# Decay attention into a gated convolution: 64-token state updates on 64x64 tiles, three whole chunks first, weights widened 128 columns at a time, and one written-out order

## The chip, the cores and the metric

The kernel runs on one core of a Trainium2 chip. The metric is device time in microseconds (us) of one execution; lower is better. The engines are named as in the profile: PE (TensorE matmul) with PEld (its weight loads), DVE (VectorE), ACT (ScalarE), POOL (GpSimd) and SP (SyncE, whose queue issues all the DMAs here).

## The reference, cut to what matters

Input: q, k, v of 4 batches x 8 heads x 768 tokens x 64 (float32), one decay `lam` per head, and a gated layer with two 512x512 float64 weights and a 5-tap float64 convolution. Tokens go in blocks of 64:

```
for b in range(nb):                                   # 12 blocks of 64
    intra = einsum('bhic,bhjc->bhij', qb, kb) * Dmask # lam**(i-j) where i >= j, else 0
    intra = einsum('bhij,bhjd->bhid', intra, vb)
    inter = einsum('bhid,bhde->bhie', qb * lam_pow, kv_state)
    out[:, :, sl] = intra + inter
    kv_state = lam_block * kv_state + einsum('bhsd,bhse->bhde', kb * rev_pow, vb)
x = out, heads side by side                           # 4 x 768 x 512
gate = sigmoid(5-tap causal convolution of x along the tokens)
result = (gate * (x @ w_val)) @ w_out
```

## The kernel before, in words

A chunk `i` is 128 tokens of two batches (`NB2`), all 8 heads. There are 12 chunks, 6 for each pair of batches; a pair's first chunk starts from an empty state and its last need not update it. For each chunk:

- **Loads** (L348): four parts of 512 KB (q and k transposed to head rows, heads 0 to 3 and 4 to 7; then v and k by token), two parts to a DMA, or one for chunk 0.
- **Scaling**: `scale_k` multiplies k by its decay (on ACT, L411, for the chunks in `K_ACT`, else on POOL, L414); `scale_q` multiplies q by the powers in `qdec` (POOL, L422).
- **scores** (L453): for each half `u` of the heads, k by q. The 128x128 triangle is cut: a 64x128 strip and a 64x64 block per head and batch, so 16 matmuls per half, on the four 64x64 tiles of the array. `mask` (DVE, L467 or L465) multiplies the scores by `dmask`.
- **intra** (L509): masked scores by v into `xp` (PSUM), in two turns; between the turns ACT reads eight columns of `xp` (`peek`, L526) and the second turn waits for that. **inter** (L489): state by scaled q into the same `xp`, 16 matmuls of 128 columns, ahead of intra.
- **outer** (L538): k by v over the 128 tokens, 16 matmuls on 128x64 tiles, into `st`; `update` (DVE, L545/L547) adds `st` and the faded state `sdec`; `fade` (POOL, L550) makes `sdec` with the power of 128.
- `keep` (ACT, L569) copies `xp` to `x` in SBUF. `x` is split into two float32r terms: `x_hi` (ACT) and `x_lo` (DVE L597 for chunks 0 and 1, else POOL L602).
- **Gate**, for two chunks together: 4 groups of 128 columns, each one tap on ACT (L629) and four on DVE (L631) in a PSUM bank, then the sigmoid (ACT, L636).
- **value** (L667): per half 24 float32r matmuls of 256 columns (w_hi by x_hi, w_hi by x_lo, w_lo by x_hi). Up to chunk 5 ACT copies the result to SBUF (L676) and DVE multiplies by the gate there (L680); from chunk 6 (`DIRECT`) DVE reads PSUM. The product `h` is split by ACT (L702) and POOL (L705).
- **project** (L728): per batch 12 matmuls of 512 columns; ACT evicts (L736), SP stores (L739).

The float64 weights are taken apart and put together as float32 by `widen`, four times on [128, 1024]: DVE cuts out exponent (L270) and mantissa (L276), ACT scales three pieces (L281, L286, L290), DVE sets the sign (L293), POOL adds (L300), DVE multiplies (L303), ACT rounds the high term (L308), POOL subtracts for the low one (L311).

Every step is given to a `Plan` with an engine, an assumed duration, a rank and its buffers. `Plan.order` plays the steps against these durations and so fixes the order in which each engine's instructions are issued; each engine's queue and SP's keep that order on the chip. PSUM has eight banks: two for the scores, two for `xp`, four (`u`) shared by everything else.

## Time and profile before

| | |
|---|---|
| runs | 231.48, 228.76, 230.7 us; median 230.7 us |
| span of the profiled execution | 228.2 us |
| PE busy | 208.8 us (91%), 3070 matmul instructions |
| DVE / ACT / POOL busy | 149.8 / 118.6 / 126.5 us |
| read from HBM, written | 29.39 MB, 6.29 MB |

The span runs from the first to the last instruction; the time of the profiled execution itself is not listed apart from the runs, which lie 0.6 to 3.3 us over its span (the median 2.5). Busy time of PE is modelled: its matmuls overlap, so start-to-start times say more than mean durations.

### The profile page before, as it was taken

To read this page: it belongs to the slowest core of one execution; us is meant where nothing else is said; L and a number is where in the kernel's file an instruction comes from. 1 tells how busy PE (TensorE), PEld (TensorE's weight loads), DVE (VectorE), ACT (ScalarE), POOL (GpSimd) and SP (SyncE) were. 2 spreads that over 40 slices of the span, in tenths; PEclk is the share of its full clock that TensorE was granted. 3 is DMA by queue.
4 is the path that set the end of the run, shared out by engine and by line. 5 is a ranking of instruction groups with operands and counts; after the bars stand their busy time and mean duration, and the time that the engine had idled before them with its cause. 6 is when DMAs were issued, how large, how long until landed. Compare 5 with 4: busy or idle time off the path is not lost.

```text
span 228.2 us, 6926 instructions
## 1 busy us (share of the span) xinstructions
PE 208.8 (91%) x3070; PEld 187.0 (82%) x3070; DVE 149.8 (66%) x201; ACT 118.6 (52%) x214; POOL 126.5 (55%) x93
## 2 busy tenths in 40 slices
PE   6786969999899999988999997989998999999994
PEld 6676868989799989987877876969897899999884
DVE  5546787999999579995389899999117931111100
ACT  2239896767945915448275356757253634121222
POOL 2045985795266599799999493343180616222210
PEclk9657879999999999999999999999999999999999
DMA  5999999928298064927121121002111111111122
GB/s 148 407 422 422 426 378 388 339 73 336 45 360 322 19 214 178 350 57 316 47 95 46 49 92 50 3 13 84 46 46 49 47 46 46 49 46 46 49 92 92
DMA packets 8238, 36.13 MB, mean 158 GB/s; under 512 B 1168, under 2 KB 1424, under 8 KB 4880
## 3 DMA queue, kind: packets, MB, share of 16 engines
q1 hardware_dynamic: 8208, 35.68, 41.1%
q8 instruction: 24, 0.39, 0.7%
q14 instruction: 6, 0.05, 0.1%
HBM read 29.39 MB, written 6.29 MB: 156 GB/s over the span
## 4 chain that ended last, share of the span: by engine, by line
PE 49%; DVE 29%; DMA 9%; POOL 6%; issue 4%; ACT 2%; SPq 0%; ACTq 0%; DVEq 0%; POOLq 0%
PE op L728 22%; PE vp L667 20%; DVE acc L631 15%; DMA ld<-in_qkv 9%; DVE g L680 6%; DVE A L467 4%; POOL qd L422 3%; POOL w_m L300 2%; PE xp L509 2%; PE xp L489 2%; PE s L453 1%; DVE state L547 1%; DVE w_m L303 1%; DVE w_m L276 1%; PE st L538 1%
## 5 line engine op out<-in xcount | busy, mean ns | idle before, releaser
L631 DVE SCALAR_TENSOR_TENSOR acc<-x,conv_sb,acc 128x512 f32<-128x512 f32 x96 | 66.4, 748 | 8.4 <-ACT acc L629 8.2
L728 PE MATMUL op<-wo_hi,hs 128*128 128x512 f32 (+1 forms) x200 | 61.5, 390 | 2.3 <-ACT seen L526 1.0
L667 PE MATMUL vp<-x_hi,wv_hi 128*128 128x256 f32 x192 | 54.7, 285 | 0.5 <-ACT g L636 0.5
L667 PE MATMUL vp<-x_lo,wv_hi 128*128 128x256 f32 x192 | 53.7, 280 | 0.3 <-POOL x_lo L602 0.2
L667 PE MATMUL vp<-x_hi,wv_lo 128*128 128x256 f32 x192 | 53.6, 279 | 0.0
L705 POOL TENSOR_TENSOR hs<-g,hs 128x512 fp32r<-128x512 f32 x24 | 32.4, 1359 | 33.7 <-ACT hs L702 30.2
L728 PEld LDWEIGHTS op<-wo_hi,hs 128*128 128x128 f32 x200 | 35.8, 188 | 10.2 <-ACT seen L526 1.1
L602 POOL TENSOR_TENSOR x_lo<-x,x_hi 128x1024 fp32r<-128x1024 f32 x10 | 24.4, 2444 | 27.9 <-ACT x_hi L593 27.9
L728 PE MATMUL op<-wo_lo,hs 128*128 128x512 f32 (+1 forms) x100 | 38.6, 386 | 0.0
L667 PEld LDWEIGHTS vp<-x_hi,wv_hi 128*128 128x128 f32 x192 | 36.0, 187 | 2.2 <-ACT g L636 1.0
L422 POOL TENSOR_TENSOR qd<-ld,qdec 128x512 f32<-128x512 f32 x20 | 30.2, 1526 | 12.7 <-DMA ld<-in_qkv 12.7
L667 PEld LDWEIGHTS vp<-x_lo,wv_hi 128*128 128x128 f32 x192 | 36.1, 188 | 1.2 <-POOL x_lo L602 0.7
L736 ACT COPY o<-op 128x512 f32<-128x512 f32 (+1 forms) x25 | 14.2, 569 | 43.8 <-PE op L728 34.5
L667 PEld LDWEIGHTS vp<-x_hi,wv_lo 128*128 128x128 f32 x192 | 36.0, 188 | 0.0
L680 DVE TENSOR_TENSOR g<-vp,g 128x512 f32<-128x512 f32 x12 | 8.3, 688 | 35.4 <-PE vp L667 30.4
L509 PE MATMUL xp<-A,ld 64*64 64x128 f32 (+1 forms) x768 | 25.2, 262 | 2.4 <-ACT seen L526 1.8
L509 PEld LDWEIGHTS xp<-A,ld 64*64 64x64 f32 x768 | 21.4, 144 | 5.4 <-ACT seen L526 2.3
L467 DVE TENSOR_TENSOR A<-s,dmask 128x768 f32<-128x768 f32 x21 | 20.0, 951 | 9.0 <-PE s L453 7.6
L636 ACT ACTIVATE g<-acc 128x512 f32<-128x512 f32 x24 | 14.4, 600 | 16.8 <-DVE acc L631 16.8
L453 PE MATMUL s<-ld 64*64 64x128 f32 (+1 forms) x672 | 19.0, 252 | 4.0 <-DMA ld<-in_qkv 2.5
L728 PEld LDWEIGHTS op<-wo_lo,hs 128*128 128x128 f32 x100 | 18.8, 188 | 4.2
L453 PEld LDWEIGHTS s<-ld 64*64 64x64 f32 x672 | 17.0, 138 | 4.9 <-DVE A L467 1.7
(59 smaller groups left out, 264.1 us busy)
## 6 DMA issues: line engine op xcount, KB each, us to landing
ld<-in_qkv SPq DMA_DIRECT2D x22, 1024.0 KB, 7.9
out<-o SPq DMA_DIRECT2D x23, 256.0 KB, 2.0
ld<-in_qkv SPq DMA_DIRECT2D x4, 512.0 KB, 6.3
w_raw<-in_w_val SPq DMA_DIRECT2D x2, 1024.0 KB, 12.4
w_raw<-in_w_out SPq DMA_DIRECT2D x2, 1024.0 KB, 12.3
...
lam_bc<-in_lam SPq DMA_DIRECT2D x1, 8.0 KB, 1.7
```

The lines of the kernel that those rows point to most:

```text
L422: nc.gpsimd.tensor_tensor(out=s["qd"][:, hs], in0=lds[i]["qT"][:, u], in1=qdec[:, hs], op=ALU.mult)
L453: nc.tensor.matmul(s["s"][b][rows(r if lo == 0 else 1 - r), at(n)], t["kT"][rows(b), u, 2 * r + n, lo:hi], t["qT"][rows(b), u, 2 * r + n, ...
L467: nc.vector.tensor_tensor(out=s["A", u], in0=s["s", u], in1=m[:, None, :].to_broadcast([P, NB2, SW]), op=ALU.mult)
L509: nc.tensor.matmul(s["xp"][rows(n), b, h // 2, lo:], lds[i]["v"][rows(r), b, h * D : (h + 1) * D], s["A", u][rows(r), b, at(n)], start=fir ...
L602: nc.gpsimd.tensor_tensor(out=s["x_lo"], in0=s["x"], in1=s["x_hi"].bitcast(F32), op=ALU.subtract)
L631: nc.vector.scalar_tensor_tensor(out=to, in0=src, scalar=w, in1=to, op0=ALU.mult, op1=ALU.add)
L636: nc.scalar.activation(xu[un]["g"][:, ct].rearrange("p u (b i) -> p b u i", b=NB2), xu[un]["acc", ct].rearrange("p b (u i) -> p b u i", u= ...
L667: nc.tensor.matmul(vp[:, f, :], w[:, ct, fs], xx[:, ct, :], start=n_mm == 0, stop=n_mm == 3 * NT - 1,)
L680: nc.vector.tensor_tensor(out=gs(u), in0=val, in1=gs(u), op=ALU.mult)
L705: nc.gpsimd.tensor_tensor(out=s["h_lo"][:, us], in0=gs(u), in1=s["h_hi"][:, us].bitcast(F32), op=ALU.subtract,)
L728: nc.tensor.matmul(op[:, cols], hh[:, ft, ts], w[:, ft, cols], start=n_mm == 0, stop=n_mm == 3 * NT - 1,)
L736: nc.scalar.copy(s["o", b, j][:, cols], s["op", b, j][:, cols])
```

## The change

The `Plan` with durations and ranks gives way to one list, `ORDER`, of 697 step names that all engines follow. In it the first half of w_val is loaded ahead of chunk 0. Five matmuls of 512 columns on a tile of zeros are added (`f.0` to `f.4`: two at the start, two ahead of chunk 0's scores, one at the very end).

Chunks 0 to 2 (`BIG`) are computed whole: 128x128 scores, the half above the diagonal multiplied by zeros of the mask, 128 tokens in one state update. The other nine work by 64 tokens: 32 score matmuls of 64x64x64, 32 of intra, two halves of inter with 16 each, 32 of outer, all on 64x64 tiles, and two state updates and two fades. The scan for `qdec` on DVE becomes seven doublings on POOL; `kdec` is dropped; `dmask` is copied out of the 128-wide mask by ACT. `peek` stays in chunk 6 alone. Chunk 0's `scale_k` moves from ACT to POOL, and the pairs' last chunks (5 and 11), which had none, get `scale_k` (POOL), half an outer, one update.

`widen` runs on [128, 512], eight times; its sum moves from POOL to DVE and into a PSUM bank, and ACT's scaling of the low word is dropped. value is issued in four steps for each chunk and project in two for each batch. From chunk 6 the gated product stays in PSUM (`H_DVE`) and its low term moves from POOL to DVE. `keep` and the early `x_hi`, `x_lo` become two instructions each.

```diff
-SLOTS = {..., "A": 3, ...}
-K_ACT = (0, 1, 2, 3, 4, 6)
-S_OWN = (0, 1, 2)
+FILL = 5
+SLOTS = {..., "A": 2, ...}
+K_ACT = (1, 2, 3, 4, 6)
+BIG = (0, 1, 2)
+H_DVE = (6, 7, 8, 9, 10, 11)
+ORDER = """
+f.0 f.1 wv.0 dm.0 qe dm.1 ld.0.0 wv.0.1.e wv.0.0.e ld.0.2 wv.1 wv.0.0.m wv.0.1.m wv.0.0.w wv.0.1.w wv.0.0.r kd.0
+wv.0.0.s f.2 f.3 s.0.0 wv.0.1.r m.0.0.0 m.0.1.0 wv.0.0.v s.0.1 m.0.1.1 m.0.0.1 wv.0.1.s wv.0.1.v wv.1.0.e ia.0.0
+ia.0.1 wv.1.1.e st.0 up.0.0 ld.1.0 s.1.1 qd.1.0 wv.0.0.h wv.0.0.l dc wv.0.1.h ld.2.0 xh.0 xl.0 x.0 wv.0.1.l fd.0.0
+m.1.1.1 qd.1.1 qd.2.1 wv.1.0.r s.1.0 m.1.0.1 m.1.1.0 m.1.0.0 wv.1.0.m wv.1.0.w wv.1.0.s s.2.1 s.2.0 wv.1.0.v wv.1.1.m
+ld.1.2 ia.1.0 ia.1.1 kd.1 wv.1.1.w in.1.0 xh.1 m.2.1.1 wv.1.0.h wo.0 m.2.0.1 wo.0.1.e wo.0.0.e wo.0.1.r cv wv.1.0.l
+m.2.0.0 cv.e cv.m wv.1.1.r cv.r st.1 hi.0 xl.1 x.1 v.0.0 up.1.0 v.0.1 wv.1.1.s wv.1.1.v v.1.0 pb.0.0 v.1.1 m.2.1.0
...
+"""
     def run(self):
-        for k in self.order():
+        for name in ORDER.split():
...
+    def make_qdec():
+        nc.gpsimd.tensor_copy(qdec_c[:, :, 0:1], lam_bc[:, :, None])
+        n = 1
+        while n < C:
+            nc.gpsimd.tensor_tensor(
+                out=qdec_c[:, :, n : 2 * n], in0=qdec_c[:, :, 0:n],
+                in1=qdec_c[:, :, n - 1 : n].to_broadcast([P, H, n]), op=ALU.mult,
+            )
+            n *= 2
...
         def float_m():
+            s["v"] = bank("w_v", [P, n]) if big else const.tile([P, n], F32, name="w_v")
+            nc.scalar.activation(s["v"], s["m"], AF.Copy, bias=1.0, scale=2.0**-20)
...
         def whole():
-            nc.gpsimd.tensor_tensor(out=s["mf"], in0=s["mf"], in1=s["r"], op=ALU.add)
+            nc.vector.scalar_tensor_tensor(
+                out=s["v"], in0=s["low"].bitcast(U32), scalar=2.0**-52, in1=s["v"], op0=ALU.mult, op1=ALU.add
+            )
         def scale():
+            s["w"] = hi if not big else s["v"] if lo_dve else s["m"].bitcast(F32)
+            nc.vector.tensor_tensor(out=s["w"], in0=s["v"], in1=s["e"].bitcast(F32), op=ALU.mult)
...
+                for k in range(W_S):                      # scores by 64 tokens
+                    u, h = us[k // HP], k % HP
+                    for m in range(2):
+                        for b in range(NB2):
+                            ms = slice(m * D, (m + 1) * D)
+                            nc.tensor.matmul(
+                                sp[b][rows(m), k, :], t["kT"][rows(b), u, h, ms], t["qT"][rows(b), u, h, ms],
+                                start=True, stop=True,
+                            )
...
+            for h in range(H):                            # outer by 64 tokens
+                hs = slice(h * D, (h + 1) * D)
+                for b in range(NB2):
+                    for m in range(n_st):
+                        nc.tensor.matmul(
+                            st[m][rows(b), h, :], lds[i]["k"][rows(m), b, hs], lds[i]["v"][rows(m), b, hs],
+                            start=True, stop=True,
+                        )
...
+            t_ia = add(f"ia.{i}.0", "PE", lambda f=intra: f(0), [*t_mask[0], ...], [xp_buf, *A_bufs, ld_buf[i]])
+                t_turn = t_read = add(f"in.{i}.0", "PE", lambda f=inter: f(0), [t_ia, t_state, *t_qd], ...)
+            t_state = add(f"up.{i}.0", "DVE", lambda f=update: f(0), [t_st, t_read, t_sdec], [st_bufs[0]])
+                t_sdec = add(f"fd.{i}.0", "POOL", fade, [t_state, *t_qdec])
+            t_read = add(f"in.{i}.1", "PE", lambda f=inter: f(1), [t_turn, t_state, *t_qd], [xp_buf, qd_buf])
+            t_in = add(f"ia.{i}.1", "PE", lambda f=intra: f(1), [t_read, *t_mask[1]], ...)
+                t_state = add(f"up.{i}.1", "DVE", lambda f=update: f(1), [t_st, t_read, t_sdec], [st_bufs[1]])
+                t_sdec = add(f"fd.{i}.1", "POOL", lambda f=fade, n=after_c: f(n), [t_state, *t_qdec])
...
+                s["h", u] = s["vp", u] if i in H_DVE else gs(u)
+                nc.vector.tensor_tensor(out=s["h", u], in0=val, in1=gs(u), op=ALU.mult)
...
+                (nc.vector if h_in else nc.gpsimd).tensor_tensor(
+                    out=s["h_lo"][:, us], in0=s["h", u], in1=s["h_hi"][:, us].bitcast(F32),
```

In `ORDER`, `s`, `ia`, `in`, `st`, `v`, `p` are scores, intra, inter, outer, value and project; `dm`, `qe`, `dc` the tables; `m`, `up`, `fd` mask, update and fade; `kd`, `qd` the scaled k and q; `x`, `xh`, `xl`, `t`, `sg`, `pb`, `ap`, `hh`, `hl`, `ev`, `o` keep, the split of x, taps, sigmoid, value's copy, the product, its split, eviction and store; `wv`, `wo`, `cv` with a letter at the end are the stages of `widen`. The first number is the chunk (or pair of chunks).

## Rows read from the trace of the kernel before

**Rows 1.** The page: the span and the engines' busy time.

```profile
span 228.2 us, 6926 instructions
...
PE 208.8 (91%) x3070; PEld 187.0 (82%) x3070; DVE 149.8 (66%) x201; ACT 118.6 (52%) x214; POOL 126.5 (55%) x93
```

**Rows 2.** Busy time by stretch (columns: stretch, sum, PE, PEld, DVE, ACT, POOL, granted PE clock, DMA share, GB/s).

```profile
10.00:20.00 10.00, 7.22 (x158) 6.81 (x158) 6.06 (x16) 6.06 (x19) 3.56 (x5) 0.61 1.01 423
...
37.90:99.00 61.10, 59.08 (x1264) 56.01 (x1256) 56.12 (x64) 39.93 (x69) 44.62 (x29) 1.00 0.60 220
99.00:149.00 50.00, 46.11 (x680) 39.15 (x680) 41.40 (x49) 27.68 (x48) 39.18 (x30) 1.00 0.23 86
149.00:225.20 76.20, 74.80 (x476) 65.51 (x476) 27.50 (x42) 28.18 (x48) 24.37 (x16) 1.00 0.14 53
```

**Rows 3.** The end of the chain that ended last, in order of time (start, us, what).

```profile
156.24 2.83 PE vp L667 x24
159.06 2.80 PE op L728 x12
...
225.23 0.37 ACT o L736
```

**Rows 4.** PE's timeline (start, us, line, form of the first instruction of the group, how many), in order: where value begins; one inter, one half of scores, one turn of intra; one outer and what follows it; the last matmuls of a turn of intra, cut at eight and at four instructions. A float32 matmul of the program is two instructions here, so x32 is 16 matmuls.

```profile
37.93 0.38 PE L667 MATMUL vp<-x_hi,wv_hi 128*128 128x256 f32 x1
...
92.95 1.10 PE L489 MATMUL xp<-qd,state 64*64 64x128 f32 x32
93.88 0.85 PE L453 MATMUL s<-ld 64*64 64x128 f32 x32
94.55 0.85 PE L509 MATMUL xp<-A,ld 64*64 64x128 f32 x32
...
81.45 1.15 PE L538 MATMUL st<-ld 128*64 128x64 f32 x32
82.54 1.10 PE L489 MATMUL xp<-qd,state 64*64 64x128 f32 x32
...
42.66 0.29 PE L509 MATMUL xp<-A,ld 64*64 64x64 f32 x8
...
42.72 0.24 PE L509 MATMUL xp<-A,ld 64*64 64x64 f32 x4
```

**Rows 5.** First uses of the loads, from the timelines of PE (scores of chunk 0 on its first 512 KB, then both halves of the scores of chunk 1), ACT (scaling of k, the first use of all 2 MB of chunk 0) and POOL (scaling of q, the first use of 1 MB of chunk 1); in brackets the idle time before and what ended it.

```profile
6.31 0.90 PE L453 MATMUL s<-ld 64*64 64x128 f32 x32 [1.51 <-DMA ld<-in_qkv]
...
12.69 1.56 PE L453 MATMUL s<-ld 64*64 64x128 f32 x32 [1.04 <-DMA ld<-in_qkv]
14.00 1.53 PE L453 MATMUL so<-ld 64*64 64x128 f32 x32
...
10.17 2.44 ACT L411 ACTIVATE ld<-ld,kdec 128x128 f32<-128x128 f32 x8 [7.94 <-DMA ld<-in_qkv]
...
12.70 2.50 POOL L422 TENSOR_TENSOR qd<-ld,qdec 128x512 f32<-128x512 f32 x2 [10.84 <-DMA ld<-in_qkv]
```

**Rows 6.** Groups by line and form over the whole span, on DVE and POOL (busy us, mean ns of one, idle before).

```profile
L631 DVE SCALAR_TENSOR_TENSOR acc<-x,conv_sb,acc 128x512 f32<-128x512 f32 x96 | 66.4, 748 | 8.4 <-ACT acc L629 8.2
...
L705 POOL TENSOR_TENSOR hs<-g,hs 128x512 fp32r<-128x512 f32 x24 | 32.4, 1359 | 33.7 <-ACT hs L702 30.2 <-PE st L538 3.5
...
L680 DVE TENSOR_TENSOR g<-val,g 128x512 f32<-128x512 f32 x12 | 17.1, 1439 | 0.1
...
L300 POOL TENSOR_TENSOR w_m<-w_m,w_raw 128x1024 f32<-128x1024 f32 x4 | 10.1, 2532 | 4.4 <-ACT w_m L286 4.4
...
L550 POOL TENSOR_TENSOR sdec<-state,qdec 128x512 f32<-128x512 f32 x8 | 9.3, 1163 | 6.6 <-DVE state L545 5.1 <-DVE state L547 1.4
L414 POOL TENSOR_TENSOR ld<-ld,kdec 128x512 f32<-128x512 f32 x8 | 9.2, 1175 | 4.5 <-PE vp L667 2.7 <-DMA ld<-in_qkv 1.9
...
L680 DVE TENSOR_TENSOR g<-vp,g 128x512 f32<-128x512 f32 x12 | 8.3, 688 | 35.4 <-PE vp L667 30.4 <-ACT acc L629 5.0
L293 DVE SCALAR_TENSOR_TENSOR w_e<-w_raw,w_e 128x1024 int32<-128x1024 int32 x4 | 8.2, 2050 | 1.4 <-ACT w_e L281 1.4
...
L276 DVE TENSOR_SCALAR w_m<-w_raw 128x1024 int32<-128x1024 int32 x4 | 4.9, 1230 | 0.0
...
L270 DVE TENSOR_SCALAR w_e<-w_raw 128x1024 int32<-128x1024 int32 x4 | 4.0, 1007 | 0.0
```

**Rows 7.** DVE's timeline: the first scans (eight: four of 128 columns, four of 64), and an early step of `widen`.

```profile
2.55 2.10 DVE L219 TENSOR_TENSOR_SCAN dmask<-lam_bc,eye 128x128 f32<-128x128 f32 x8 [1.54 <-DMA lam_bc<-in_lam]
...
22.21 1.46 DVE L293 SCALAR_TENSOR_TENSOR w_e<-w_raw,w_e 128x1024 int32<-128x1024 int32 x1 [0.77 <-ACT w_e L281]
```

**Rows 8.** PE's groups by line and form from 37.9 to 225.2 us, those of attention: how many of its instructions are left there, and the idle time before them.

```profile
L509 PE MATMUL xp<-A,ld 64*64 64x128 f32 x288 | 14.1, 278 | 1.5 <-ACT seen L526 1.5
L453 PE MATMUL s<-ld 64*64 64x128 f32 x256 | 12.0, 274 | 1.5 <-DVE A L467 1.5
...
L489 PE MATMUL xp<-qd,state 64*64 64x128 f32 x256 | 8.8, 275 | 0.0
L538 PE MATMUL st<-ld 128*64 128x64 f32 x192 | 7.1, 225 | 1.2 <-ACT g L636 1.2
```

**Rows 9.** PE's longest waits for ACT (us in total, times, longest).

```profile
PE xp L509 <- ACT seen L526: 1.8, 3, 0.8
```

**Rows 10.** The gate's product on DVE with both inputs in SBUF (count: min/median/max ns, first and last start).

```profile
L680 DVE TENSOR_TENSOR g<-val,g x12: 677/832/4432, 52.5 to 132.9; 128x512 f32<-128x512 f32 x12
```

More of the change, by code (lines that the diff above doesn't have):

```diff
@@ new lines, in cut_dmask, with widen @@
+    def cut_dmask():
+        for m in range(2):
+            nc.scalar.copy(dmask[rows(m)], mask_c[rows(m), :, m * D : (m + 1) * D])
+    t_mask_c = [add(f"dm.{u}", "DVE", lambda u=u: make_dmask(u)) for u in range(2)]
+    t_dmask = [add("dc", "ACT", cut_dmask, t_mask_c)]
+    t_qdec = [add("qe", "POOL", make_qdec)]
+    def widen(name, after, take, make, n, hi, lo):
+        s = {}
+        big = lo is not None
+        bufs = [Buf("val")] if big else []
+        v_bufs = [Buf("u")] if big else []
+        lo_dve = name in W_DVE
@@ L326, in widen, with on @@
+        def on(what, e, fn, after, v=False):
+            return add(f"{name}.{what}", e, fn, after, [*bufs, *take, *(v_bufs if v else ())])
+        t_e = on("e", "DVE", parts, after)
+        t_mf = on("m", "ACT", float_m, [t_e], v=True)
+        t_relu = on("r", "ACT", relu, [t_e])
+        t_w = on("w", "DVE", whole, [t_mf], v=True)
+        t_s = on("s", "DVE", sign, [t_relu])
+        t_v = on("v", "DVE", scale, [t_w, t_s], v=True)
+        if not big:
             return [t_v]
-        t_hi = on("ACT", 900, high, [t_v])
@@ L328, in widen @@
-        return [t_hi, on("POOL", 2250, low, [t_hi])]
+        t_hi = on("h", "ACT", high, [t_v], v=lo_dve)
+        return [t_hi, on("l", "DVE" if lo_dve else "POOL", low, [t_hi], v=lo_dve)]
     lds = {}
@@ L471, in decay_attention_then_gated_conv @@
[L471 to L486 removed]
+                shape = [HP, C] if big else [H, D]
@@ new lines, in intra_c @@
+        def intra_c(u, i=i, s=s, first=first):
+            if u == 0:
+                s["xp"] = bank("xp", [P, NB2, NP, C], "xp")
+            for g in range(NP // 2 * u, NP // 2 * (u + 1)):
+                for b in range(NB2):
+                    for hh in range(2):
+                        h = 2 * g + hh
+                        nc.tensor.matmul(
+                            s["xp"][rows(hh), b, g, :], lds[i]["v"][:, b, h * D : (h + 1) * D],
+                            s["A", u][:, b, h - HP * u, :],
+                            start=g == 0, stop=first and g == NP - 1, skip_group_check=True,
+                        )
@@ L535, in outer, with peek @@
+        def peek(s=s):
+            nc.scalar.copy(seen, s["xp"][:, :, 0, :, 0])
+        n_st = 1 if last or big else 2
+        st_bufs = [Buf("u") for _ in range(n_st)]
+        def outer(i=i, s=s, n_st=n_st, big=big):
+            st = s["st"] = [bank("st", [P, H, D]) for _ in range(n_st)]
+            if big:
                 for h in range(H):
@@ L554, in decay_attention_then_gated_conv, with update @@
[L554 to L556 removed]
+        def update(m, s=s, first=first):
+            if first and m == 0:
+                nc.vector.tensor_copy(state, s["st"][m])
+            else:
+                nc.vector.tensor_tensor(out=state, in0=s["st"][m], in1=sdec, op=ALU.add)
```

653 lines of the change are left out of this document (296 added, 357 removed).

## The prediction

> **What bounds the kernel now.** I read the page first: PE is busy for 91% of a span of 228.2 us, and the two engines behind it are far lower [rows 1]. Busy PE is modelled, so the second view is the end of the chain of waits: from 156 us on, blocks of value (24 matmuls, 2.83 us) and of project (12 matmuls, 2.80 us) follow each other, and only an eviction and a store come after them [rows 3]. All 24 blocks of each kind therefore cost 24 x (2.83 + 2.80) = 135.1 us, which this change leaves alone. The third view is PE's timeline: the first value matmul starts only at 37.93 us [rows 4]. The last project ends at 225.2 us, where its eviction takes over [rows 3]; 228.2 - 225.2 = 3.0 us of tail follow.
>
> Between these two points lie 187.3 us. Attention fills part of them. From start to start, one half of scores takes 94.55 - 93.88 = 0.67 us, one turn of intra has the same columns, inter 93.88 - 92.95 = 0.93 us, outer 82.54 - 81.45 = 1.09 us [rows 4]. After 37.9 us there are 8 chunks of scores (256 instructions of the wide form, 32 a chunk), 9 of intra, 8 inters and 6 outers [rows 8]: 8 x 1.34 + 9 x 1.34 + 8 x 0.93 + 6 x 1.09 = 36.8 us. So 135.1 + 36.8 = 171.9 us is work and 15.4 us is lost in changes of tile form and in waits. PE is the bound from 37.9 us to the end; before that it is short of work. DVE comes second and not by much: it is busy for 56.12 of 61.10 us up to 99 us and for 41.40 of 50 us after that [rows 2].
>
> The question is then: when can value begin, what PE work is left at that point, and who keeps PE waiting in between.
>
> **PE's work by 64 tokens.** A half of scores is 16 matmuls, eight of 128 and eight of 64 columns: 1536 columns in 0.67 us, 0.436 ns each with four 64x64 tiles at work. By 64 tokens scores are 32 matmuls of 64 columns, 2048 columns or 0.89 us a chunk instead of 1.34; intra the same; inter keeps its columns (0.89, in two halves); outer comes to 0.89 instead of 1.09, and pays no change of form. That assumes that short matmuls keep the rate per column. They do: the last eight of a turn of intra, all of 64 columns, start at 42.66 us and the last four at 42.72, so four of them take 0.06 us, 15 ns each [rows 4]. The Trainium skill speaks against this (TensorE: Matmul & The Clock Gate, Part 1): it puts a floor of about 25 ns under the distance of two matmuls, however short. By it 64 instructions would take 1.6 us and not 0.89. The row here is below that floor, and I go by the row; the other case is a rival below.
>
> Whole chunks (0 to 2) go the other way: a half of scores is eight matmuls of 128 columns on two tiles, 1024 columns at twice 0.436 ns, 0.89 us instead of 0.67; intra likewise.
>
> **When value can begin.** The loads set the pace. Chunk 0's first 512 KB are used at 6.31 us, its 2 MB at 10.17, one MB more at 12.70 [rows 5]: 2.53 us a MB after 5.1 us. On SP's queue the new order is half of w_val, chunk 0 (two transfers), the other half, q/k of chunk 1, q/k of chunk 2, v/k of chunk 1. They land at 7.6, 10.2, 12.7, 15.2, 17.8, 20.3 and 22.8 us. So chunk 0 waits 2.5 us for a weight that it doesn't need, as the price of widening early. Ahead of the first value stand, on PE, chunks 0 and 1 and the scores of 2. The last load to matter is v/k of chunk 1: from 22.8 us, intra 1.8, inter 0.93, outer 1.09 give 26.6 us, with k scaled by ACT in 2.44 us beside intra. That is the early bound, 27 us.
>
> The late bound comes from DVE. Up to the last mask of chunk 1 it has 8 scans (2.10 us for four long and four short [rows 7]; 8 long 2.8 by their columns), 4 pairs of exponent and mantissa at half of 1.007 + 1.230 (1.12 us), two sums, signs and products of `widen`, 8 masks, an update, an x_lo. Prices: the sum has one input in SBUF and one in PSUM, as a tap has, 0.69 us (66.4 over 96); the sign is half of 2.05, 1.03 us; product, masks and updates read one PSUM operand of 512 columns, 0.69 us [rows 6]; x_lo is two such, 1.4. Together 2.8 + 4.5 + 4.8 + 5.5 + 0.7 + 1.4 = 19.7 us from 2.55, and it must wait for w_val between 5.4 and 7.6: 24.5 us. With 2 us more of waiting, and with PE at half clock, as it was in the stretch from 10 to 20 us (0.61 granted [rows 2], a half of scores in 14.00 - 12.69 = 1.31 us [rows 5]), intra, inter and outer take 7.6 us and value starts at 34. The fills cost 4 x 0.9 us, or twice that at half clock; they sit ahead of chunk 0's scores, where PE waits for its load until 10.2 us anyhow, and lose at most 2 us; the fifth runs beside the last store. I take 29.5 us, nearer the early bound, because the new order gives PE work before chunk 0. That is 8.4 us earlier than 37.93.
>
> **What is left then.** Value and project 135.1. Nine chunks by 64 tokens: scores and intra 18 x 0.89, 17 halves of inter 7.6, nine outers 8.0 (the two half ones run on two tiles only and cost the same): 31.6. Chunk 2: intra 1.8, inter 0.93, outer 1.09. Sum 170.5 us, against 171.9 before. So PE's total hardly falls; what is gained per small chunk is spent on whole chunks and on the two last outers, and the gain must come from the earlier start.
>
> **Who makes PE wait.** The 15.4 us lost before lose 1.8 us, the waits for `peek` [rows 9]; eleven of the twelve peeks are gone. Changes of form stay: 43 against 41. New waits come from DVE. Between value's start and the second update of chunk 3, PE has nine quarters of value, chunk 2's intra, inter and outer, two scores and half a small chunk: 12.7 + 3.8 + 1.8 + 1.8 = 20.1 us. DVE, from the last mask of chunk 1 to that update, has 3 pairs, 4 sums, 4 signs, 4 products, 8 masks, 3 updates, an x_lo, 12 taps, the small conversion: 3.4 + 2.8 + 4.1 + 2.8 + 5.5 + 2.1 + 1.4 + 8.3 + 0.7 = 31.1 us, so it gets there at 24.5 + 31.1 = 55.6 us when PE could be there at 29.5 + 20.1 = 49.6. That is 6.0 us. Queued behind the inter that waits are value of chunk 2 and the rest of chunk 3. Lost in all: 15.4 - 1.8 + 6.0 = 19.6 us.
>
> **The other edits at nothing.** POOL loses four sums (4 x 2.53) and twelve low terms (12 x 1.36), 26.4 us, and gains nine fades (10.5), three scalings of k (7.1) and the doublings (1024 columns, twice a fade, 2.3, to 4 with eight starts): a few us less than 126.5 [rows 1, 6], hidden as before; uncovered, a fade would cost 1.16 us for each of 17 updates. ACT loses a pass over the weights and a k scaling; it was busy 52%. The stores that the list puts late, and loads behind them on SP, run in a stretch with a DMA share of 0.23 or less [rows 2]. From chunk 6 the low term goes to DVE, 12 x 0.69 = 8.3 us, where DVE is busy 27.5 of 76.2 us [rows 2]. The product then holds one of the four shared banks for 2.83 us of value and three passes of about 0.7: 5 us, two banks at PE's pace, so nothing; with outer taking two banks instead of one, a group of taps could wait for a bank, at most an outer and two updates, 2.3 us a chunk in DVE's queue, and I keep that for the first rival.
>
> DVE's price has an end that the sum doesn't show. With both inputs in SBUF the gate's product took 677 to 4432 ns, with one in PSUM 688 on average [rows 6, 10]. The Trainium skill (SBUF — State Buffer, Who interferes with whom) says that a DVE operation with two SBUF inputs and a POOL operation that reads SBUF exclude each other for their whole length; the trace agrees by this spread. It makes the sign and the product up to chunk 5 the uncertain ones; `widen`'s sum and product leave that class.
>
> **Sum.** 29.5 + 170.5 + 19.6 + 3.0 = 222.6 us of span against 228.2. The runs lie 0.6 to 3.3 us over the span, the median 2.5; with 1.9 added, between the middle and the two ends, I predict 224.5 us.
>
> **Rivals.**
> - *DVE is the bound, and it is not faster.* Up to the first update of chunk 7 DVE has 8 scans 2.8, `widen` 8 x 3.53 = 28.2, 24 masks 16.6, 11 updates 7.6, x_lo 2.8, 0.7, 48 taps 33.1 and 10 gate products at their mean before, 1.44 [rows 6], 14.4: 106.2 us from 2.55. PE has, from the inter behind it, 26 quarters of value (36.8), project 50.4, 9 halves each of inter and intra 8.0, outer and scores 5.3: 100.5 us. With the tail 212.3. DVE idled 13.6 of 111 us between 37.9 and 149 us [rows 2]; at that rate over the 86 us after chunk 1's masks 12, plus 2.2 for w_val and 2 at the start, plus 2 on PE: 230.5 us of span, 232.4 us. For it: the two sums are equal along the whole middle, so each wait there counts. Against: with products at 0.69 and signs at half of 1.46 [rows 7] it is 10 us less. It decides where DVE's waits and exclusions before that update exceed 14 us.
> - *The start isn't gained.* Value starts at 35 us, by the late bound and a `scale_k` behind `widen` on ACT: 5.5 us more, 228 us of span, 230 us: the same as before.
> - *The waits vanish.* Value at 27.5, DVE's exclusions mostly gone, lost 13: 214 us of span, 216 us.
> - *Short matmuls hit a floor.* At 1.6 us instead of 0.89 for 64 instructions, 9 x 4 groups less three halves: 0.71 x 34 = 24 us, 247 us. The 0.06 us for four [rows 4] speak against it.
>
> **The numbers.** Forecast 0.50 (its own range 219 to 228); waits vanish 0.12; start not gained 0.17; DVE the bound 0.18; the floor 0.03. Range 215 to 234: it leaves some 0.06 below and 0.12 above. About 1% is what a measurement tells from no change here, 228.4 to 233.0 us. Faster: 0.50 + 0.12 = 0.62; same 0.18; slower 0.20.
>
> **What would show it.** Right: the first value matmul near 29.5 us; a 64-token group of scores, 64 instructions, in about 0.9 us; waits of PE on DVE's updates between 40 and 60 us; value and project back to back at the end. Wrong: value after 33 us, or PE idle for more than 20 us behind it; DVE busy without a gap up to 130 us would mean the first rival. A total under 216 us would say that I overrate DVE's waits.

## The result, and the profile after

The changed kernel takes 213.96 us (median of 5 runs, 213.86 to 217.46), the kernel before beside it 230.59 us: a ratio of 0.9325 [0.9265, 0.9384], 6 to 7% faster. The forecast was 224.5 us with a range of 215 to 234; the direction was right and the gain was underrated by some 10 us. Ratios are taken from the fast runs alone and medians from all, so where the two differ the text goes by the ratio.

In the execution that was profiled first (span 215.7 us) the granted clock of TensorE was 0.65 between 20 and 29.7 us, so the profile shown here is that of a second execution of the unchanged kernel, the run e1_same_again below: span 211.7 us, clock 1.00 in every stretch shown. In the first one value started at 29.74 us, by luck where the forecast had it.

Page of the changed kernel, the span and the busy times (against [rows 1]):

```profile
span 211.7 us, 7772 instructions
...
PE 203.0 (96%) x3464; PEld 180.1 (85%) x3464; DVE 156.2 (74%) x240; ACT 114.5 (54%) x218; POOL 114.4 (54%) x103
```

Busy time by stretch (stretch, sum, PE, PEld, DVE, ACT, POOL, granted clock, DMA share, GB/s; against [rows 2]):

```profile
10.00:20.00 10.00, 6.12 (x112) 5.29 (x109) 9.96 (x19) 5.71 (x12) 5.98 (x6) 1.00 1.02 428
20.00:26.30 6.30, 5.92 (x128) 5.38 (x128) 5.52 (x12) 3.89 (x12) 3.77 (x3) 1.00 1.01 419
26.30:99.00 72.70, 71.83 (x1578) 65.67 (x1575) 67.24 (x104) 54.63 (x113) 53.62 (x46) 1.00 0.58 213
99.00:149.00 50.00, 50.00 (x1090) 43.31 (x1090) 39.30 (x54) 25.53 (x43) 37.46 (x30) 1.00 0.44 150
149.00:208.67 59.67, 59.67 (x520) 54.09 (x519) 27.10 (x39) 20.74 (x36) 9.67 (x6) 1.00 0.13 47
```

From the first value matmul on, PE is busy for 181.5 of 182.4 us. Up to 99 us DVE is nearly as full, 67.24 of 72.70 us. What is left for PE to wait for is little. PE's waits (us in total, times, longest) came to 7.2 us from 37.9 us to the end in the kernel before, when the rows of that view are added up; its three largest are

```profile
PE xp L509 <- ACT seen L526: 1.5, 2, 0.8
PE s L453 <- DVE A L467: 1.5, 2, 1.1
PE st L538 <- ACT g L636: 1.2, 1, 1.2
```

In the changed kernel these are all of them, from 26.3 us to the end:

```profile
PE op L767 <- ACT val L713: 0.3, 1, 0.3
PE vp L704 <- DVE w_em L270: 0.3, 1, 0.3
PE op L767 <- DVE state L550: 0.2, 1, 0.2
```

PE's timeline (start, us, line, form of the first of a group, how many): the stretch up to the first value matmul; a 64-token outer and what follows it; chunk 3's second inter.

```profile
19.89 1.16 PE L431 MATMUL so<-ld 64*128 64x128 f32 x16 [1.74 <-DMA ld<-in_qkv]
...
22.33 1.97 PE L496 MATMUL xp<-A,ld 128*64 128x128 f32 x32 [0.38 <-DMA ld<-in_qkv]
24.23 1.10 PE L507 MATMUL xp<-qd,state 64*64 64x128 f32 x32
25.26 1.15 PE L535 MATMUL st<-ld 128*64 128x64 f32 x32
26.34 0.39 PE L704 MATMUL vp<-x_hi,wv_hi 128*128 128x256 f32 x1
...
45.47 1.11 PE L543 MATMUL st<-ld 64*64 64x64 f32 x64
46.41 0.65 PE L518 MATMUL xp<-qd,state 64*64 64x64 f32 x32
48.61 0.69 PE L518 MATMUL xp<-qd,state 64*64 64x64 f32 x32
```

Value starts at 26.34 us instead of 37.93 [rows 4], 11.6 us earlier. The end of the chain of waits (start, us, what) is value and project back to back, as in [rows 3]; only the fifth fill stands behind the last project, beside the store:

```profile
174.59 14.39 PE vp L704 x120
...
193.24 15.43 PE op L767 x78
208.67 0.86 PE fill L189 x2
```

By the terms of the prediction the span is then 26.3 (start) + 170.5 (work listed) + 11.8 (lost, 208.67 - 26.34 - 170.5) + 3.0 (tail) = 211.7 us, against 29.5 + 170.5 + 19.6 + 3.0 = 222.6 us. The start was 3.2 us too late in the forecast, and the loss 7.8 us too large. In the same terms the kernel before is 37.93 + 171.9 + 15.4 + 3.0 = 228.2 us: of the 16.5 us gained between the two profiles the start gives 11.6, the loss 3.6 and the listed work 1.4.

DVE's groups by line and form (busy us, mean ns | idle before), the scans (min/median/max ns, first and last start), and three lines of its timeline: the last of chunk 1's masks, the step behind them at 20.10 us, and the update that lets chunk 3's second inter go.

```profile
L461 DVE TENSOR_TENSOR A<-s,dmask 128x512 f32<-128x512 f32 x18 | 12.1, 682 | 1.2 <-PE s L441 1.2
...
L258 DVE SCALAR_TENSOR_TENSOR w_em<-w_raw,w_em 128x512 int32<-128x512 int32 x8 | 5.7, 714 | 0.8 <-ACT w_em L250 0.8
L270 DVE TENSOR_TENSOR w_em<-w_v,w_em 128x512 f32<-128x512 f32 x8 | 5.5, 690 | 0.2
...
L241 DVE TENSOR_SCALAR w_em<-w_raw 128x512 int32<-128x512 int32 x8 | 4.4, 547 | 0.0
```

```profile
L199 DVE TENSOR_TENSOR_SCAN mask_c<-lam_bc,ident x8: 395/435/1194, 2.4 to 5.3; 128x128 f32<-128x128 f32 x8
```

```profile
18.91 1.28 DVE L454 TENSOR_TENSOR A<-s,mask_c 128x512 f32<-128x512 f32 x2
20.10 0.69 DVE L264 SCALAR_TENSOR_TENSOR w_v<-w_raw,w_v 128x512 f32<-128x512 uint32 x1
...
47.63 0.68 DVE L552 TENSOR_TENSOR state<-st,sdec 128x512 f32<-128x512 f32 x1
```

DVE is done with chunk 1's masks at 20.1 us where the late bound had 24.5, and with the update at 48.3 us where the forecast had 55.6. PE comes to the inter behind it at 48.61 us and doesn't wait: the two meet almost exactly.

### The profile page after: what moved, and what is told of

The parts are those of the page before. It is cut to its first block, busy times and chain, and to the rows that moved or that the text cites. A ratio compares the mean times of both kernels' runs of the same rounds, so it can differ in the third digit from the quotient of the medians.

```text
span 215.7 us, 7772 instructions
## 1 busy us (share of the span) xinstructions
PE 207.8 (96%) x3464; PEld 183.7 (85%) x3464; DVE 158.2 (73%) x240; ACT 114.5 (53%) x218; POOL 114.1 (53%) x103
## 4 chain that ended last, share of the span: by engine, by line
PE 69%; DVE 14%; POOL 6%; issue 5%; ACT 4%; DMA 1%; ACTq 0%; DVEq 0%; POOLq 0%
PE vp L704 25%; PE op L767 23%; DVE acc L665 5%; PE xp L481 3%; PE xp L518 3%; PE xp L496 3%; PE fill L189 2%; PE st L543 2%; DVE A L454 2%; PE s L441 2%; POOL x_lo L639 2%; PE warm L167 2%; POOL qd L397 2%; PE s L431 1%; DVE g L718 1%
## 5 line engine op out<-in xcount | busy, mean ns | idle before, releaser
L665 DVE SCALAR_TENSOR_TENSOR acc<-x,conv_sb,acc 128x512 f32<-128x512 f32 x96 | 71.2, 754 | 6.4 <-ACT acc L663 4.2
L704 PE MATMUL vp<-x_hi,wv_hi 128*128 128x256 f32 x192 | 55.8, 291 | 0.0
L397 POOL TENSOR_TENSOR qd<-ld,qdec_c 128x512 f32<-128x512 f32 (+1 forms) x18 | 22.4, 1257 | 3.6 <-PE xp L518 3.6
L555 POOL TENSOR_TENSOR sdec<-state,qdec_c 128x512 f32<-128x512 f32 x17 | 18.5, 1091 | 7.6 <-DVE state L552 7.6
L744 POOL TENSOR_TENSOR hs<-g,hs 128x512 fp32r<-128x512 f32 x12 | 15.4, 1293 | 11.9 <-ACT hs L741 11.9
L552 DVE TENSOR_TENSOR state<-st,sdec 128x512 f32<-128x512 f32 x17 | 11.7, 687 | 12.1 <-PE st L543 7.5
L605 ACT COPY x<-xp 128x512 f32<-128x512 f32 x24 | 12.9, 590 | 10.6 <-PE xp L481 7.5
L741 ACT CAST hs<-vp 128x512 fp32r<-128x512 f32 x12 | 7.0, 590 | 18.9 <-DVE vp L718 18.8
L663 ACT ACTIVATE acc<-x,conv_sb 128x512 f32<-128x512 f32 x24 | 16.2, 689 | 0.6
L381 POOL TENSOR_TENSOR ld<-ld,dmask 128x512 f32<-128x512 f32 x12 | 12.9, 1101 | 6.3 <-DMA ld<-in_qkv 6.3
```

Of the source, the lines that this page charges most:

```text
L381: nc.gpsimd.tensor_tensor(out=kv[:, b], in0=kv[:, b], in1=k_mask.to_broadcast([P, H, D]), op=ALU.mult)
L397: nc.gpsimd.tensor_tensor(out=s["qd"][:, hs, ms], in0=lds[i]["qT"][:, u].rearrange("p h (m i) -> p h m i", m=2)[:, :, ms], in1=qdec[:, hs, ...
L555: nc.gpsimd.tensor_tensor(out=sdec, in0=state, in1=qdec_c[:, :, n - 1 : n].to_broadcast([P, H, D]), op=ALU.mult)
L605: nc.scalar.copy(*blocks(s["x"], b))
L663: nc.scalar.mul(to, src, w)
L665: nc.vector.scalar_tensor_tensor(out=to, in0=src, scalar=w, in1=to, op0=ALU.mult, op1=ALU.add)
```

## The experiments

Three theories of the 10 us that the forecast missed: (a) the cut of value into four steps and of project into two, which the prediction costed at nothing, gives PE something to do in each wait; (b) DVE is cheaper than its mean prices before, above all because `widen`'s sum and product have left SBUF; (c) the order of the loads alone brings the early start. The rivals are that DVE's cost doesn't matter (PE would have waited little anyway), and that the smaller pieces need no new order.

In the table "waits" are the rows of PE's waits view, from the first value matmul to the end, added up. Medians compare within a group that shares a "before"; across groups go by the ratio. The first profile's ratio was 0.9325 and the repetition's is 0.9407; 0.937 is their middle. Not every later start belongs to its edit alone: the granted clock was 0.85 to 0.80 from 10 to 40 us in e4, 0.83 from 10 to 30 us in e5, 0.83 from 20 to 30 us in e6, and 0.75 from 10 to 20 and 0.91 from 20 to 30 us in e7, against 1.00 in e1.

| run | median us | before us | ratio | first value us | waits us |
|---|---|---|---|---|---|
| (before) | | 230.7 | 1 | 37.93 | 7.2 |
| e1_same_again | 214.11 | 230.22 | 0.9407 [0.9363, 0.9451] | 26.34 | 0.8 |
| e2_no_fills | 215.64 | 230.22 | 0.9489 [0.9394, 0.9584] | 30.34 | 0.9 |
| e3_whole_blocks | 221.91 | 230.22 | 0.9779 [0.9715, 0.9843] | 26.65 | 7.1 |
| e4_masks_twice | 236.96 | 230.22 | 1.0336 [1.0214, 1.0457] | 36.29 | 10.2 |
| e5_sum_on_pool | 231.17 | 228.27 | 1.0124 [1.0086, 1.0162] | 32.27 | 9.0 |
| e6_low_on_pool | 218.27 | 228.27 | 0.9541 [0.9494, 0.9589] | 27.84 | 3.7 |
| e7_weights_after_chunk0 | 220.88 | 228.27 | 0.9682 [0.9627, 0.9738] | 32.16 | 1.8 |
| e8_before_early_weights | 248.65 | 228.27 | 1.0897 [1.0838, 1.0955] | 25.61 | 22.8 |
| e9_two_taps_fewer | 213.09 | 228.99 | 0.9285 [0.9217, 0.9353] | 26.36 | 2.0 |
| e10_second_half_later | 217.41 | 228.99 | 0.9479 [0.9418, 0.954] | 27.12 | 3.3 |
| e11_before_fine_cut | 233.85 | 229.45 | 1.0237 [1.0152, 1.0323] | 37.83 | 8.4 |
| e12_before_both | 238.19 | 229.45 | 1.0417 [1.0342, 1.0493] | 27.55 | 12.5 |

**e1, the changed kernel again**, unedited.

> The changed kernel once more, nothing edited, for a second profile. In the first one the granted PE clock fell to 0.65 between 20 and 29.7 us, and its span (215.7 us) was 3.6 us over that of the other runs (212.1). Theory 'start and slack': time is the start of value plus 170.5 us of work plus some 12 us lost plus 3 us of tail; so with the clock full up to value, value starts near 26 us instead of 29.74 and the span is near 212. Rival 'the loss is elsewhere': value starts near 29.7 again and the 3.6 us are missing after it.

214.11 us. Value starts at 26.34 us and the span is 211.7, as theory 'start and slack' had it. It gives the profile above, and the spread between two groups of runs: 0.9325 and 0.9407.

**e2, without the fills**

```diff
-FILL = 5
+FILL = 0
```

> The five matmuls on zeros are taken out, of the constant and of the list; all else stays. Theory 'clock': the fills keep PE's clock up through the wait for chunk 0; without them the clock falls before 10 us, chunks 0 and 1 run at half rate (11 us of work at full rate ahead of value), value starts 4 to 8 us later and the time is 4 to 8 us longer. Theory 'start and slack' with the loads as the pace: chunk 0 and 1 wait for loads and DVE anyhow, so value starts 0 to 3 us later and the time follows by the same amount.

1.5 us more than e1 at the median, with intervals that overlap: not told apart in time. In the profiled run PE did nothing from 5.06 us until the first scores at 9.00, and the granted clock fell (columns as above):

```profile
0.00:10.00 10.00, 5.01 (x26) 4.82 (x28) 7.00 (x17) 3.49 (x6) 3.93 (x14) 0.91 0.80 287
10.00:20.00 10.00, 8.67 (x124) 8.18 (x120) 9.36 (x16) 3.91 (x8) 5.66 (x5) 0.75 1.01 425
20.00:26.30 6.30, 5.16 (x52) 4.80 (x54) 5.66 (x8) 4.95 (x13) 3.82 (x4) 0.64 1.02 425
```

Value then starts at 30.34 us, and the waits behind it stay at 0.9 us. Little of that later start is shown to be the fills'. PE's timeline has the first scores here and with the fills (e1), then the first scores of chunk 2 here and in the first profile of the unchanged kernel, which has all fills:

```profile
9.00 2.08 PE L431 MATMUL s<-ld 64*128 64x128 f32 x16 [3.94 <-DMA ld<-in_qkv]
...
8.64 1.16 PE L431 MATMUL s<-ld 64*128 64x128 f32 x16 [0.38 <-DMA ld<-in_qkv]
...
20.55 1.16 PE L431 MATMUL so<-ld 64*128 64x128 f32 x16 [1.89 <-DMA ld<-in_qkv]
...
19.93 1.65 PE L431 MATMUL so<-ld 64*128 64x128 f32 x16 [1.89 <-DMA ld<-in_qkv]
```

Chunk 2's scores begin 0.66 us later than in e1 (19.89), and from there to value it takes 9.79 us here and 29.74 - 19.93 = 9.81 in the first profile, with a granted clock of 0.66 and 0.65 behind 20 us, against 6.45 in e1 at 1.00. So the larger part of the delay also came about with the fills, and what they are worth stays open.

**e3, value and project in whole blocks.** In the order, each `v.i.0` stands directly ahead of its `v.i.1`, `v.i.2` ahead of `v.i.3`, and each pair of `p` steps likewise:

```diff
-... x.1 v.0.0 up.1.0 v.0.1 wv.1.1.s wv.1.1.v v.1.0 pb.0.0 v.1.1
+... x.1 up.1.0 v.0.0 v.0.1 wv.1.1.s wv.1.1.v pb.0.0 v.1.0 v.1.1
```

> The list alone is changed: each half of value and each batch's project is issued in one piece again (its first step moved down to stand right ahead of its second), all else in the same order. If the small waits of PE behind value's start (some 3.5 us in all, against 9 before) are owed to the finer cut, that is, work put into the gaps where DVE's updates are awaited, the loss grows by 3 to 6 us. If they are owed to DVE's passes being cheaper than the forecast had them, the time stays within 1.5 us.

221.91 us, 7.8 more than e1 on the same chip and more than either theory expected. The profiled run, at a clock of 1.00 like e1's, spans 218.0 us, 6.3 more, with the start 0.3 us later and PE's waits back at 7.1 us, which are 6.3 us more:

```profile
PE xp L518 <- issue: 1.9, 1, 1.9
PE xp L518 <- ACT seen L524: 1.8, 1, 1.8
PE xp L518 <- DVE state L552: 0.9, 1, 0.9
PE vp L704 <- DVE state L552: 0.8, 1, 0.8
```

The first and the third lie where the forecast put its 6.0 us, at chunk 3's two inters: before the last instruction of the first, at 49.03 us, and before the second, at 50.15 us (PE's timeline, then DVE's update between the two, with the idle time before them):

```profile
49.03 0.27 PE L518 MATMUL xp<-qd,state 64*64 64x64 f32 x1 [1.87 <-issue]
50.15 0.69 PE L518 MATMUL xp<-qd,state 64*64 64x64 f32 x32 [0.85 <-DVE state L552]
...
49.40 0.69 DVE L552 TENSOR_TENSOR state<-st,sdec 128x512 f32<-128x512 f32 x1 [1.79 <-PE xp L518]
```

In the changed kernel a quarter of chunk 2's value stands between these inters. The 1.87 us are put to "issue": the profile shows nothing that PE waited for there, and DVE's update stood idle until that inter was done, so it isn't DVE that caused them. Only the 0.85 us is a wait for DVE's update. So theory (a) holds for this order: with the blocks whole PE waits 6.3 us more, 1.9 us of it without a cause that the profile shows.

**e4, every mask twice.** DVE does 30 passes more, each writing the same values again.

```diff
-nc.vector.tensor_tensor(out=s["A"][:, b, hs], in0=s["s", us][b], in1=dmask[:, hs], op=ALU.mult)
+for _ in range(2):
+    nc.vector.tensor_tensor(out=s["A"][:, b, hs], in0=s["s", us][b], in1=dmask[:, hs], op=ALU.mult)
```

> Every mask multiplication of the scores is done twice on DVE (30 more passes of 128x512 from PSUM, 0.60 us each from start to start: 18 us, of which 14 us fall before the first update of chunk 7); the values are the same. Theory 'slack': DVE was busy 63.6 of 69.3 us between 29.7 and 99 us and only 40 of 50 us after, so up to 99 us some 6 us are free; PE waits for the rest: 4 to 8 us longer, and the end is back to back again. Rival 'DVE co-bound', the forecast's: DVE's work up to chunk 7 and PE's behind it add up to the span, so all 14 us show: 12 to 15 us longer. Rival 'DVE doesn't matter': under 2 us.

236.96 us, by the ratios some 21 us more than e1 (0.093 of 228) and 20.8 between the two profiles, where the highest theory had 15. DVE is busy 23.1 us longer (179.3 us against 156.2). Half of the time is the start, 36.29 instead of 26.34 us, the other half PE's waits behind it, 10.2 instead of 0.8. Of the view over the whole span the second row lies behind value's start, the other two ahead of it:

```profile
PE xp L498 <- DVE A L455: 3.9, 3, 2.4
PE vp L706 <- DVE w_em L270: 2.9, 1, 2.9
PE s L431 <- DVE A L455: 2.8, 1, 2.8
```

More DVE work costs nearly its full length, with the lower clock of the start in it. DVE stands at the limit, as the prediction's first rival had it, but with a time far below that rival's 232.4 us.

**e5, `widen`'s sum back on POOL, in SBUF**, with ACT's scaling of the low word.

```diff
-s["v"] = bank("w_v", [P, n])
+s["v"] = s["m"].bitcast(F32)
+s["r"] = s["low"].bitcast(F32)
+nc.scalar.mul(s["r"], s["low"].bitcast(U32), 2.0**-52)
...
+nc.gpsimd.tensor_tensor(out=s["v"], in0=s["v"], in1=s["r"], op=ALU.add)
```

> One part undone: widen's sum of the eight weight pieces goes back to POOL, in SBUF and in place, with ACT's scaling of the low word in front of it; DVE loses 8 passes of 0.60 us (4.8 us), POOL gains 8 of about 1.3 us, ACT 8 of about 0.6; the product on DVE then has two inputs in SBUF again. Theory 'DVE's prices': moving sum and product into a PSUM bank was what made DVE's passes cheap; undone, the products are drawn out by POOL (from 0.69 us to 1 us or more each), POOL's queue delays the first weight, value starts 1 to 4 us later and the time is 2 to 6 us longer. Rival 'count of passes': DVE is co-bound, so 4.8 us less work on it makes the kernel up to 4 us faster.

231.17 us, ratio 1.0124: the whole gain is gone (228.27 x 0.937 = 213.9, so +17 us, where 2 to 6 were expected), although DVE loses eight passes. Its product now reads two SBUF inputs beside POOL's traffic and waits for POOL's sum (DVE's group, columns as above; then one product in DVE's timeline and the two sums on POOL beside it):

```profile
L278 DVE TENSOR_TENSOR w_em<-w_em 128x512 f32<-128x512 f32 x8 | 13.1, 1639 | 8.2 <-POOL w_em L270 7.9
...
27.32 1.76 DVE L278 TENSOR_TENSOR w_em<-w_em 128x512 f32<-128x512 f32 x1 [1.22 <-POOL w_em L270]
...
26.00 2.54 POOL L270 TENSOR_TENSOR w_em<-w_em,w_raw 128x512 f32<-128x512 f32 x2 [0.48 <-ACT w_em L260]
```

1639 ns instead of 690 for the same pass. The product shown ends at 29.08 us, 0.54 us after POOL's sum (28.54), and seven of the eight end 0.54 to 0.55 us after the POOL operation beside them. The Trainium skill (SBUF — State Buffer, Who interferes with whom) says that such a DVE operation and a POOL operation that reads SBUF exclude each other; these rows agree. Value starts at 32.27 us, and PE waits 9.0 us behind it, 2.9 of them at "issue", without a cause that the profile shows. So theory (b) holds for the price of the pass and for the start. How the 17 us divide between that price, the wait for POOL's sum, an order that was made for sums on DVE, and a lower clock (0.83 also from 40 to 60 us) isn't shown.

**e6, the low term of the product back on POOL**

```diff
-H_DVE = (6, 7, 8, 9, 10, 11)
+H_DVE = ()
```

> One part undone: from chunk 6 the gated product goes to SBUF and its low term is made on POOL (12 passes of 1.3 us) instead of DVE (12 of 0.6 us). Value's start stays. Theory 'the end is PE's': behind chunk 6 DVE has room (40 of 50 us, then 17 of 29, 12 of 34.5), so its relief brings nothing; the chain from value to project grows by 0.7 us for each half, which the list covers except at the end: 0 to 2 us longer. Rival 'DVE co-bound to the end': up to 5 us faster.

218.27 us, ratio 0.9541, about 4 us more than the changed kernel (0.937 x 228.27 = 213.9). The profiled run starts value 1.5 us later, but the edit changes nothing ahead of chunk 6, so that is the lower clock of that run. PE now waits 2.3 us for POOL's `x_lo` (not at all in e1, but 1.1, 1.7 and 0.5 us in e7, e9 and e10, which leave the low term on DVE too) and 0.8 for POOL's low term. The move of the low term to DVE, costed at nothing, is thus worth up to 3 us; 0 to 2 were expected.

**e7, weights behind chunk 0**

```diff
-f.0 f.1 wv.0 dm.0 qe dm.1 ld.0.0 wv.0.1.e wv.0.0.e ld.0.2 wv.1 wv.0.0.m ...
+f.0 f.1 dm.0 qe dm.1 ld.0.0 ld.0.2 wv.0 wv.0.1.e wv.0.0.e wv.1 wv.0.0.m ...
```

> The list alone is changed: on SP's queue the first half of w_val goes behind chunk 0 instead of ahead of it, and the two exponent steps that need it stay first on DVE behind the scans. Chunk 0 lands 2.5 us earlier, the weight 5 us later, and DVE, in its fixed order, stands until 12.7 us instead of 6.4. Theory 'start': value starts 3 to 6 us later and the time follows one to one, since loss and work behind it stay. Rival 'loads don't matter': the start of value is set by v/k of chunk 1, whose place in the queue is the same, and the time stays within 1 us.

220.88 us, ratio 0.9682, 7 us more, a little over the 3 to 6 of the first theory. Value starts 5.8 us later, at 32.16, and the waits behind it hardly change (1.8 us): the start passes into the time about one to one. DVE's row names the cause, and PE's the price:

```profile
DVE w_em L241 <- DMA w_raw<-in_w_val: 4.8, 1, 4.8
```

```profile
PE xp L496 <- DVE A L454: 5.6, 2, 5.4
```

**e8, the kernel before with the weights early**, through the old planner's ranks alone.

```diff
-RANK = {..., "wv": 1.5, "half": 1.0, ...}
+RANK = {..., "wv": -12, "half": 4.0, ...}
```

> The kernel before, with two ranks changed so that its planner loads the first half of w_val ahead of chunk 0 and widens it first (and orders the rest anew by its own rule). If the earlier start is what the change is worth, value starts near 28 us instead of 37.93 and the time falls by 6 to 9 us, to 222 or so. If the start can only be used together with the finer cut and the written-out order, value starts early but the waits behind it grow, and the time falls by 0 to 4 us.

248.65 us, 9% slower than before, outside both expectations. Value starts at 25.61 us, even earlier than in the changed kernel, but with less attention done. Of PE's groups of attention from there to the end two are (as in [rows 8])

```profile
L509 PE MATMUL xp<-A,ld 64*64 64x128 f32 x352 | 17.7, 281 | 1.2 <-ACT seen L526 1.2
L453 PE MATMUL s<-ld 64*64 64x128 f32 x288 | 14.8, 293 | 7.5 <-DVE A L467 7.5
```

that is 11 chunks of intra and 9 of scores instead of 9 and 8; with 10 inters and 8 outers instead of 8 and 6, 8.1 us of work at the prediction's prices (1.34, 1.34, 0.93 and 1.09 us) have moved behind the start. And PE's waits behind it grow from 7.2 to 22.8 us, most of them for DVE:

```profile
PE s L453 <- DVE A L467: 7.5, 8, 1.3
PE op L728 <- DVE g L680: 6.4, 1, 6.4
```

Theory (c) falls as a cause by itself: the early start is needed (e7), but in the old planner's order it doesn't pay. Whether it would pay in the kernel before under a written-out order, no run shows.

**e9, two taps fewer.** This kernel leaves out the last two taps of the convolution, 48 DVE passes.

```diff
+if kk > 2:
+    return
```

> Left out: the last two of the five taps of the convolution (48 of DVE's passes, 0.67 us each, 32 us). All else stays, the list too. If DVE still holds PE up behind value's start, the time falls by 3 us or more. If the list hides DVE wholly, so that it is at its limit but not over it, only the small waits go: 0 to 1.5 us shorter, with value starting where it did (26.3 us, no tap comes before that).

213.09 us, ratio 0.9285: 0.004 and 0.012 below the two results of the changed kernel; the intervals overlap with the first and not with the second. DVE's busy time falls from 156.2 to 123.2 us and the time by 1 to 3 us at most. So the limit has two sides: more DVE work costs nearly in full (e4), less brings little, since PE is full.

**e10, the second half of w_val later**, an attempt at a better version: `wv.1` and the stages of its two pieces behind v and k of chunk 1 (`ld.1.2`).

```diff
-... ld.0.2 wv.1 wv.0.0.m ... ld.1.2 ia.1.0 ia.1.1 kd.1 wv.1.1.w ...
+... ld.0.2 wv.0.0.m ... ld.1.2 wv.1 ia.1.0 ia.1.1 kd.1 wv.1.0.e wv.1.1.e ...
```

> The list alone is changed, as a try at a better version: the second half of w_val is loaded behind chunk 1 and the scores of chunk 2 instead of ahead of them, and its widening steps move behind chunk 1's masks on DVE and ACT. Chunk 1's last load lands 2.5 us earlier (near 20 us), so value can start 2 to 2.5 us earlier. Theory 'start': the time falls by 1.5 to 2.5 us, to about 212. Rival 'DVE co-bound': DVE does the same work in another order and stands idle while it waits for chunk 1, so value starts earlier but its next steps wait for x_lo and the second half: between 1 us shorter and 2 us longer.

217.41 us, ratio 0.9479, 2 to 3 us more than the middle; the interval overlaps with e1's, but the two profiles, both at a clock of 1.00, differ by 3.6 us. Value starts 0.8 us later instead of earlier, and the widening now falls where PE wants DVE and a PSUM bank (over the whole span):

```profile
PE s L431 <- DVE A L454: 1.8, 1, 1.8
...
PE vp L704 <- DVE w_em L270: 1.3, 1, 1.3
```

No version that computes everything and beats the changed kernel came out of these runs.

**e11, the kernel before with the finer cut alone**, laid out by the old planner.

```diff
-def value(u=u, s=s):
+def value(f0, u=u, s=s):
...
-for f in range(HU):
+for f in (f0,):
...
-def project(b=b, j=j, s=s, cols=cols):
+def project(u, b=b, j=j, s=s, cols=cols):
...
-for ft in range(NT):
+for ft in range(HU * u, HU * (u + 1)):
```

> The kernel before with one edit: value is cut into four steps for each chunk and project into two for each batch, laid out by the old planner; everything else (widths of chunks, widening, loads) as before. Theory: putting value and project together in the changed kernel cost 7.8 us, so the smaller pieces are worth something by themselves where a planner may put attention between them: 4 to 7 us less than before, 223 to 227 us, from fewer waits of PE behind the first value (9.2 us before), with value starting at 37.9 us as before. Rival: the cut pays only together with an order written out against measured times, and the old planner, whose durations are assumed, gives at most 2 us: 228 to 231 us.

233.85 us, ratio 1.0237: some 5 us slower than before, outside both expectations. Waits rise from 7.2 to 8.4 us, and the changes of tile form behind the first value, counted in PE's timeline, from the 41 of the prediction to 51. The planner changes form more often and fills nothing. In its order the finer cut by itself is worth less than nothing.

**e12, the finer cut and the early weights together**, in the kernel before: the edits of e8 and e11.

> The kernel before with that finer cut and, through the planner's ranks, w_val loaded and widened early (the ranks that took the kernel before from 228.3 to 248.7 us with the old cut). Attention, DVE's passes, POOL's sums and the low-word scaling are as before. Theory: value begins near 25.6 us, but DVE's mixed passes in SBUF and the four POOL sums are still there, so PE goes on waiting for DVE; the smaller pieces fill some of the 27 us of stalls, and the time comes to 236 to 245 us. Rival: the stalls were only due to the coarse pieces, and then the early start is kept: 212 to 222 us.

238.19 us, ratio 1.0417, as the theory expected. Against e8 the pieces do fill waits (22.8 to 12.5 us, and 1.0897 to 1.0417 in the ratio), but with attention, DVE's SBUF passes and POOL's sums as before it stays slower than before. The early start is not kept, and as in e8 it comes with 8.1 us more attention behind it.

## Why the prediction was wrong, step by step

**The step that failed is "Who makes PE wait": "Lost in all: 15.4 - 1.8 + 6.0 = 19.6 us".** It measured 11.8. Of the waits, 7.2 us before, it kept 5.4 and added 6.0, so 11.4; the view now shows 0.8. With value and project in whole blocks, as the prediction priced them, it shows 7.1 (e3). So of the 10.6 us of waits that didn't come, 6.3 go with the finer cut and 4.3 weren't there without it either. Two things are behind it.

- *An edit was left out.* "Value is issued in four steps for each chunk and project in two" stands in the change and has no price in the prediction. Put back into whole blocks, the waits return to 7.1 us and the time by 6.3 us between the profiles, 7.8 at the median (e3). At the inter where the 6.0 us were forecast only 0.85 us is then a wait for DVE's update; 1.87 us at the inter before it have no shown cause. The runs also bound the claim: by the old planner the same cut costs some 5 us (e11). How much of e3's loss is due to an order made for quarters, and not made anew for halves, stays open.
- *DVE was priced too high.* The prediction added up mean durations, but a pass starts before the one ahead of it has ended: masks last 0.68 us on average and start 0.60 us apart, and exponent and mantissa start 0.67 us apart as a pair instead of the 1.12 taken. The sign averages 0.71 us instead of 1.03, a mean that held long passes (1.46 us in one early step against 2.05 on average for 1024 columns, [rows 6, 7]). The wait of 2.2 us for w_val didn't come, since DVE goes on to it at 6.38 us, right behind the scans. Only the scans went the other way, 4.02 us instead of 2.8: the last of them are drawn out to 1194 ns beside the doublings that the change puts on POOL. So DVE was done with chunk 1's masks 4.4 us earlier than forecast and reached the update 7.3 us earlier, 48.3 instead of 55.6 (the text calls it the second update of chunk 3; what it lists ends at the first, the one that the second inter waits for). e5 shows the other price of that step: with the sum and product in SBUF the gain is gone.

What lies outside the waits grew, from 15.4 - 7.2 = 8.2 us to 11.0: a block of value takes 14.39 / 5 = 2.88 us instead of 2.83 (1.2 us over 24), a 64-token group 46.41 - 45.47 = 0.94 instead of 0.89 (1.4 us over 27). That partly hid the error.

**The start was a term mis-sized: 29.5 us forecast, 26.34 measured.** The early bound had it: v and k of chunk 1 at 22.8 us (used at 22.33), then intra, inter and outer, 26.6 us. I moved away from it because of DVE's late bound, 24.5 us for chunk 1's masks; they were done at 20.1; that bound also had PE at half clock ahead of value, where 1.00 was granted in e1. The over-pricing of DVE stands behind both errors. The first profile doesn't bear the forecast out, though value starts at 29.74 us there: it got there by a clock of 0.65, not by DVE, and its loss is 212.61 - 29.74 - 170.5 = 12.4 us, not 19.6.

**Right:** the start is the lever and counts one to one (e7). The rate of short matmuls held: 64 in 0.94 us. The Trainium skill's floor of about 25 ns (TensorE: Matmul & The Clock Gate, Part 1) would make 1.6 us, an estimate; this trace disagrees with it again. The tail is 3.0 us as forecast, and the listed work hardly moved. A run's time lies 1.8 us over its span (217.46 against 215.7 us in the first profile), where 1.9 was added. The sign "a total under 216 us would say that I overrate DVE's waits" came, and the runs agree with it. What the fills are worth wasn't told apart (e2).

**Wrong in part among the edits at nothing:** the low term's move is worth up to 3 us (e6), since with the low term on POOL, PE waits longer for POOL's `x_lo`.

**The rivals.** "The waits vanish" (value at 27.5, lost 13, 216 us) is the case that came, and its chance of 0.12 was too low. "DVE is the bound" names the right neighbour: DVE is nearly full up to 99 us, and 23.1 us more of it cost some 21 (e4). "The start isn't gained" and "the floor" fell.

**What no run shows:** none takes back the updates by 64 tokens or the three whole chunks, and none lays out the changed kernel by the old planner. What these parts of the change are worth by themselves stays open.
